# Constant columns written ahead of the loads, mask building reordered, and attention of batch 1 spread over ch1 and ch2 of batch 0

## The chip, the cores and the metric

The kernel runs on one core of a Trainium2 chip. The metric is the device time of one launch in microseconds (us). Each kernel was launched several times, and the median is quoted. A profile is one of those launches, recorded by the hardware profiler. The span in a profile is about 2 us shorter than the time of the same launch, so spans are compared with spans and times with times.

Engine names in profile lines: PE is TensorE (matmul), PEld its weight loads, DVE VectorE, ACT ScalarE, POOL GpSimd (here it issues the loads) and SP SyncE (it issues the stores).

## The reference

Eight batches, eight heads, 576 positions, head size 64: causal attention over a window of 128 positions with a distance bias, then an MLP mixer on the result. Inputs and outputs are float32.

```python
rel = pos[:, None] - pos[None, :]
mask = (rel >= 0) & (rel < 128)
attn = softmax(where(mask, scale * q @ k.T - slope * |rel|, -1e9))
x = (attn @ v)                                  # (batch, 576, 512)
h = np.maximum(xt @ w_tok1, 0.0) @ w_tok2       # xt: x transposed
u = x + h.transpose(0, 2, 1)
out = u + np.maximum(u @ w_ch1, 0.0) @ w_ch2    # d_ch = 1536
```

## The kernel before

Attention works on pairs of heads, four pairs to a batch, so batch 1 is pairs 4 to 7. A pair takes three steps. `att_T` transposes q and k on TensorE and copies both out of PSUM. `att_S(g, half)` makes scores, `exp` on ScalarE, and multiplies by a mask on VectorE (tile `pb`). `att_V` multiplies by v; v carries a column of ones, so the softmax sum comes with it, and VectorE divides (tile `xb`). All three take their PSUM tiles from one pool of two. `regroup(b, ...)` rearranges q and k of a batch on VectorE before its transposes.

The mixer of a batch is `tok1`, `tok2` (result `ub`), transposes (`ut`, copied to `UT`), `ch1` (24 groups of four matmuls, each followed by a Relu on ScalarE) and `ch2`. `mixer_items(b)` holds ch2 of batch b-1 and the rest of batch b. `spread(main, side)` interleaves two lists by cost.

```python
    with tc.manual_schedule():          # every engine keeps this order
        dma_qk(0, 0, 2)                 # GpSimd issues the loads: q, k, v of batch 0,
        ...                             # weights, q and k of batch 1, v of batch 1
        nc.vector.memset(patT[0 : P - TAIL, :], 0.0)
        nc.vector.memset(W1[0 : P - TAIL, NF, :], 0.0)
        nc.vector.memset(vp[0][0 : P - TAIL, NF, :, 0:D], 0.0)
        build_consts()
        regroup(0, 0, 2)
        build_bias()
        build_masks(0)
        att_T(0, True)
        regroup(0, 2, 4)
        att_S(0, 0)
        att_T(1, True)
        nc.vector.memset(vp[0][:, :, :, D : D + 1], 1.0)      # ones column, batch 0
        build_masks(1)
        ...                             # the other pairs of batch 0
        nc.vector.memset(vp[1][0 : P - TAIL, NF, :, 0:D], 0.0)
        nc.vector.memset(vp[1][:, :, :, D : D + 1], 1.0)      # ones column, batch 1

    with tc.manual_schedule(engines={ENG.PE}):   # only TensorE keeps this order
        its = mixer_items(0)
        n = len(its) - NHT
        run(its[:n])                    # mixer 0 up to the 12th ch1 group
        regroup(1, 0, H)
        ...
        side = []
        for g in range(NHP, 2 * NHP):   # batch 1: T and S, no V
            side.append((0.6, lambda g=g: att_T(g)))
            side.append((0.5, lambda g=g: att_S(g, 0)))
            side.append((0.5, lambda g=g: att_S(g, 1)))
        spread(its[n:], side)           # over the last 12 ch1 groups
        its = mixer_items(1, lead=3)
        run(its[:6])
        spread(its[6:9], [(0.6, lambda g=g: att_V(g)) for g in range(NHP, 2 * NHP)])
        its = its[9:]
        side = [(0.6, lambda: att_T(2 * NHP)), (0.6, lambda: att_T(2 * NHP + 1))]
        side += [(0.5, lambda: att_S(2 * NHP, 0)), (0.5, lambda: att_S(2 * NHP, 1))]
        for g in range(2 * NHP, 3 * NHP):
            side += att_step(g)         # T of pair g+2, S of g+1, V of g
        spread(its, side)
        ...                             # batches 2 to 8: spread(mixer_items(b), att_steps)
```

In the second block a scheduler puts the work of the other engines in order, so the place of an instruction on VectorE has to be looked up in the built program.

The softmax here doesn't subtract the row's maximum and nothing guards it: scores larger than these inputs give would overflow.

## Time and profile before

| kernel before | |
|---|---|
| median time | 357.11 us (356.5 to 357.9) |
| first tok1 matmul | 39.94 us |
| first ch1 matmul | 51.30 us |
| start of mixer 2 | 126.86 us |
| from there to the end | 229.6 us of a span of 356.5 |

The times within the span are starts of the named matmuls in the timeline. From mixer 2 on, TensorE has next to no waits (38.27 us busy of the 38.60 us from 127 to 165.6), so there was little to win there.

The table of busy time by stretches gives the middle of the kernel, from the first ch1 to mixer 2. After the stretch and its length come the busy time of each engine (with its instructions), the mean granted TensorE clock (the share of its full speed that the chip allowed), the DMA share and GB/s.

```profile
core 0: us, PE busy (x) PEld busy (x) DVE busy (x) ACT busy (x) POOL busy (x), PEclk, DMA share, GB/s
51.30:126.86 75.56, 63.72 (x637) 40.80 (x636) 37.43 (x61) 45.16 (x94) 8.13 (x10) 0.91 0.60 84
```

TensorE is busy 63.7 of 75.6 us, at a clock of 0.91.

The timeline of VectorE shows the start. Columns: start, duration, engine, line, operation, output<-input, and in brackets the idle time before it and what ended it.

```profile
16.65 0.43 DVE L169 COPY masks<-patB 128x512 bf16<-128x512 bf16 x1 [6.76 <-DMA vp_91<-in_v_dram]
16.78 0.09 DVE L505 MEMSET vp_91<- 128x40 bf16 x1
33.53 0.96 DVE L145 COPY qg<-qn_86 96x3072 bf16<-96x3072 bf16 x1 [6.65 <-DMA qn_86<-in_q_dram]
36.20 0.95 DVE L145 COPY kg<-kn_88 96x3072 bf16<-96x3072 bf16 x1 [0.39 <-DMA kn_88<-in_k_dram]
39.06 0.82 DVE L295 TENSOR_TENSOR xb<-ot,rt 128x640 bf16<-128x640 f32 x1
48.59 0.73 DVE L347 TENSOR_TENSOR ub<-ht,xb 128x512 bf16<-128x512 f32 x1 [1.33 <-DMA vp_92<-in_v_dram]
48.72 0.09 DVE L529 MEMSET vp_92<- 128x40 bf16 x1
```

The masks at 16.65 us need no load. They stand behind the ones column of `vp_91`, which had to wait for the loads into the same tile. (The profile starts the ones column 0.13 us after the masks; in the order of this block, which every engine keeps, it comes first.) In the same way the fourth `ub` addition, at 48.59 us, stands behind the ones column of `vp_92` (0.09 us of work), which waited for v of batch 1. Between them lies the regroup of batch 1, which waits for q and k. The chain of waits puts the two large DMA waits on the critical path:

```profile
17.65 13.00 DMA WC_105<-in_moe_w_ch_dram
31.58 16.84 DMA vp_92<-in_v_dram
```

The timeline of TensorE shows the waits of the middle stretch:

```profile
51.30 8.00 PE L371 MATMUL ct<-UT,WC_105 128*128 128x288 bf16 x52
61.34 0.39 PE L244 MATMUL sp<-qTz_93,kT_97 64*128 64x256 bf16 x4 [1.03 <-DVE kT_97 L222]
66.17 0.39 PE L244 MATMUL sp<-qTz_94,kT_98 64*128 64x256 bf16 x4 [1.92 <-DVE kT_98 L222]
71.01 0.39 PE L244 MATMUL sp<-qTz_95,kT_99 64*128 64x256 bf16 x4 [1.92 <-DVE kT_99 L222]
77.76 0.39 PE L244 MATMUL sp<-qTz_96,kT_100 64*128 64x256 bf16 x4 [2.29 <-DVE kT_100 L222]
92.51 1.24 PE L330 MATMUL t_971<-xb,W_103 128*128 128x512 bf16 x5 [1.78 <-DVE xb L295]
105.55 0.29 PE L356 MATMUL ut<-swap,ub 128*128 128x128 bf16 x1 [2.67 <-DVE ub L347]
126.86 0.39 PE L393 MATMUL o_1494<-ident,UT 128*128 128x128 bf16 x4
```

The first and the last line are the first ch1 and the start of mixer 2. The scores of each pair wait for the copy of its k, because T and S of one pair follow each other with only one ch1 group between.

### The profile page before, as it was taken

To read this page: it belongs to the slowest core of one execution; us is meant where nothing else is said; L and a number is where in the kernel's file an instruction comes from. 1 tells how busy PE (TensorE), PEld (TensorE's weight loads), DVE (VectorE), ACT (ScalarE), POOL (GpSimd) and SP (SyncE) were. 2 spreads that over 40 slices of the span, in tenths; PEclk is the share of its full clock that TensorE was granted. 3 is DMA by queue.
4 is the path that set the end of the run, shared out by engine and by line. 5 is a ranking of instruction groups with operands and counts; after the bars stand their busy time and mean duration, and the time that the engine had idled before them with its cause. 6 is when DMAs were issued, how large, how long until landed. Compare 5 with 4: busy or idle time off the path is not lost.

```text
span 356.5 us, 6716 instructions
## 1 busy us (share of the span) xinstructions
PE 310.6 (87%) x2816; PEld 190.8 (54%) x2816; DVE 180.1 (51%) x342; ACT 178.8 (50%) x373; POOL 59.5 (17%) x79
## 2 busy tenths in 40 slices
PE   2271768579779999999999999999999999999995
PEld 1051336345437754676457645674577457745842
DVE  5292450453587548733694368534953275326012
ACT  3462007760356963286439642784378425711810
POOL 8961250020401041004000400013000000000000
PEclk9999989969998999999999999999999999999999
DMA  7999999128903692905790391009110111002022
GB/s 95 129 179 205 190 139 201 16 31 162 98 32 41 94 82 59 180 31 36 92 158 35 25 104 59 31 2 97 41 52 0 31 59 61 2 31 73 16 61 89
DMA packets 59502, 27.76 MB, mean 78 GB/s; under 512 B 38672, under 2 KB 54864, under 8 KB 59472
## 3 DMA queue, kind: packets, MB, share of 16 engines
q0 software_dynamic: 54224, 17.90, 50.7%
q1 hardware_dynamic: 5248, 9.44, 7.8%
q8 instruction: 22, 0.36, 0.5%
q14 instruction: 8, 0.07, 0.1%
HBM read 35.78 MB, written 9.44 MB: 127 GB/s over the span
## 4 chain that ended last, share of the span: by engine, by line
PE 73%; DMA 8%; DVE 8%; POOL 5%; issue 3%; ACT 2%; POOLq 0%; DVEq 0%
PE ct L371 27%; DMA vp_92<-in_v_dram 5%; PE sp L244 5%; PE ot L287 4%; DMA WC_105<-in_moe_w_ch_dram 4%; PE tT L204 3%; PE ut L360 2%; DVE ub L347 2%; PE ht L343 2%; POOL vp_91 L137 2%; DVE kg L145 1%; PE o_829 L399 1%; DVE kT_100 L222 1%; ACT pe L258 1%; POOL kn_87 L119 1%
## 5 line engine op out<-in xcount | busy, mean ns | idle before, releaser
L371 PE MATMUL ct<-UT,WC_105 128*128 128x288 bf16 x768 | 107.8, 291 | 0.2
L258 ACT ACTIVATE pe<-sp,biascol 128x512 bf16<-128x512 f32 x128 | 81.3, 692 | 28.1 <-PE sp L244 28.0
L376 ACT ACTIVATE R_102<-ct 128x288 bf16<-128x288 f32 x192 | 73.8, 423 | 40.0 <-PE ct L371 34.1
L371 PEld LDWEIGHTS <-WC_105 128*128 128x128 bf16 x768 | 72.1, 99 | 23.4 <-issue 3.9
L265 DVE TENSOR_TENSOR pb<-pe,masks 128x1024 bf16<-128x1024 bf16 x64 | 44.0, 689 | 60.9 <-ACT pe L258 60.7
L399 PEld LDWEIGHTS <-R_102 128*128 128x128 bf16 x432 | 39.6, 98 | 42.9 <-issue 2.6
L287 PEld LDWEIGHTS <-pb 128*128 128x128 bf16 x576 | 23.5, 103 | 12.1 <-issue 7.2
L347 DVE TENSOR_TENSOR ub<-ht,xb 128x512 bf16<-128x512 f32 x40 | 25.9, 682 | 7.0 <-PE ht L343 5.7
L131 POOL DMA_DIRECT2D vp_92<-in_v_dram x16 | 14.2, 899 | 77.1 <-PE ot L287 70.1
L295 DVE TENSOR_TENSOR xb<-ot,rt 128x640 bf16<-128x640 f32 x32 | 26.4, 824 | 1.0
L343 PE MATMUL ht<-r1t,W_104 128*128 128x512 bf16 x80 | 21.7, 379 | 1.6 <-DVE ub L347 1.1
L204 PEld LDWEIGHTS <-qg 96*128 96x128 bf16 x192 | 12.2, 103 | 19.2 <-DVE qg L145 14.3
L287 PE MATMUL ot<-vp_91,pb 128*128 128x65 bf16 x288 | 13.7, 209 | 7.8 <-DVE xb L295 6.6
L131 POOL DMA_DIRECT2D vp_91<-in_v_dram x12 | 10.5, 889 | 44.4 <-PE ot L287 40.3
L330 PEld LDWEIGHTS <-W_103 128*128 128x128 bf16 x80 | 7.9, 103 | 13.1 <-issue 6.2
L365 DVE COPY UT<-ut 128x576 bf16<-128x576 bf16 x32 | 13.2, 452 | 2.4 <-PE ut L360 2.3
L215 ACT COPY qTz_96<-tT 128x576 bf16<-128x576 bf16 x7 | 4.5, 639 | 18.2 <-PE tT L204 18.1
L343 PEld LDWEIGHTS <-W_104 128*128 128x128 bf16 x80 | 7.3, 98 | 11.0 <-issue 3.9
L215 ACT COPY qTz_93<-tT 128x576 bf16<-128x576 bf16 x7 | 4.5, 639 | 15.5 <-PE tT L204 15.3
L204 PE MATMUL tT<-ident,qg 96*128 96x96 bf16 x168 | 12.0, 208 | 0.0
L204 PE MATMUL tT<-ident,kg 96*128 96x96 bf16 x168 | 11.9, 208 | 0.0
L222 DVE COPY kT_97<-tT 128x576 bf16<-128x576 bf16 x7 | 5.3, 758 | 13.0 <-ACT qTz_93 L215 13.0
(186 smaller groups left out, 367.6 us busy)
## 6 DMA issues: line engine op xcount, KB each, us to landing
out_dram<-obt SPq DMA_DIRECT2D x32, 256.0 KB, 2.0
qn_86<-in_q_dram POOLq DMA_DIRECT2D x4, 576.0 KB, 9.7
kn_88<-in_k_dram POOLq DMA_DIRECT2D x4, 576.0 KB, 11.6
vp_92<-in_v_dram POOLq DMA_DIRECT2D x16, 128.0 KB, 5.2
qn_85<-in_q_dram POOLq DMA_DIRECT2D x3, 576.0 KB, 6.8
kn_87<-in_k_dram POOLq DMA_DIRECT2D x3, 576.0 KB, 9.9
WC_105<-in_moe_w_ch_dram POOLq DMA_DIRECT2D x3, 512.0 KB, 10.1
WC_106<-in_moe_w_ch_dram POOLq DMA_DIRECT2D x1, 1536.0 KB, 23.7
```

The lines of the kernel that those rows point to most:

```text
L131: nc.gpsimd.dma_start(out=vp[b % 2][:, c, :, 0:D], in_=v[b, :, c * P : (c + 1) * P, :].rearrange("h s d -> s h d"),)
L204: nc.tensor.transpose(tt[n][:, j * RP : (j + 1) * RP], t_raw[:RP, j, 2 * hp : 2 * hp + 2, :].rearrange("p h d -> p (h d)"), ident[:RP, :RP],)
L244: nc.tensor.matmul(sp[:, hh, i * 256 + x0 : i * 256 + x1], lhsT=kt[r, k0 : k0 + P], rhs=qz[r, 0, q0 : q0 + x1 - x0], start=True, stop=True,)
L258: nc.scalar.activation(out=pe[:, i, :].rearrange("p (k x) -> p k x", k=2), in_=sp[:, i, :].rearrange("p (k x) -> p k x", k=2) if ROW_TILED ...
L265: nc.vector.tensor_tensor(out=pb[:, :, :], in0=pe[:, :, :], in1=masks[:, half, 2 * hp : 2 * hp + 2, :], op=ALU.mult,)
L287: nc.tensor.matmul(ot[:, i, qb * (D + 1) : (qb + 1) * (D + 1)], lhsT=pb[:, i, col : col + P], rhs=vb[:, kc, h, :], start=(n == 0), stop=(n ...
L295: nc.vector.tensor_tensor(out=xb[b][:, :, 2 * hp * D : (2 * hp + 2) * D].rearrange("p c (i d) -> p i c d", i=2), in0=o4[:, :, :, 0:D], in1 ...
L343: nc.tensor.matmul(ht[:, :], lhsT=W2[:, j, c0(c) : c0(c) + P], rhs=r1s[b, j][:, :], start=(j == 0), stop=(j == NDH - 1),)
L347: nc.vector.tensor_tensor(out=ubs[b][:, c, :], in0=ht[:, :], in1=xb[b][:, c, :], op=ALU.add)
L371: nc.tensor.matmul(ct[:, :], lhsT=WC1[:, cb, ht_i * P : (ht_i + 1) * P], rhs=UT[:, cb, o : o + SH], start=(cb == 0), stop=(cb == NCB - 1),)
L376: nc.scalar.activation(out=R2[:, ht_i, o : o + SH], in_=ct[:, :], func=ACT.Relu)
L399: nc.tensor.matmul(o2[0][:, :], lhsT=R2[:, ht_i, col : col + P], rhs=WC2[:, ht_i, :], start=(ht_i == 0 and c != NF), stop=(ht_i == NHT - 1),)
```

## The change

Its intent: no VectorE instruction that needs no data should stand behind one that does, and batch 1's attention should run as the same pipeline as later batches' (T two pairs ahead, S one ahead, then V). Cut to its core; a branch of the kernel that was never taken was also removed, and the loads of q and k are given out one batch earlier, which leaves GpSimd's order unchanged except that q and k of batch 2 come before v of batch 2.

```diff
     with tc.manual_schedule():
+        for i in range(2):
+            nc.vector.memset(vp[i][:, :, :, D : D + 1], 1.0)
+            nc.vector.memset(vp[i][0 : P - TAIL, NF, :, 0:D], 0.0)
+        nc.vector.memset(W1[0 : P - TAIL, NF, :], 0.0)
+        nc.vector.memset(patT[0 : P - TAIL, :], 0.0)
         dma_qk(0, 0, 2)
 ...
-        (the same memsets, one by one, among the pairs of batch 0 and after them)
         build_consts()
         regroup(0, 0, 2)
         build_bias()
+        att_T(0, True)
         build_masks(0)
-        att_T(0, True)
         regroup(0, 2, 4)
         att_S(0, 0)
         att_T(1, True)
         build_masks(1)
-        regroup(0, 4, 6)
         att_S(0, 1)
+        regroup(0, 4, 6)
         att_S(1, 0)
         att_T(2, True)
         build_masks(2)
-        regroup(0, 6, 8)
         att_S(1, 1)
-        att_V(0)
+        regroup(0, 6, 8)
 ...     (V of pairs 0 and 1 one step later each)
     with tc.manual_schedule(engines={ENG.PE}):
-        (run mixer 0; T and S of batch 1; run ch2; V of batch 1)
+        its0, its1 = mixer_items(0), mixer_items(1, lead=3)
+        n0, n1 = len(its0) - NHT, 9
+        run(its0[:n0])
+        side = [(0.0, lambda: regroup(1, 0, H))]
+        if B > 3:
+            side.append((0.0, lambda: dma_qk(3, 0, H)))
+        for g in range(NHP - 2, 2 * NHP):
+            side += att_step(g, NHP)
+        spread(its0[n0:] + its1[:n1], side)
         side = []
         for g in range(2 * NHP, 3 * NHP):
             side += att_step(g)
+        spread(its1[n1:], side)
```

More of the change, by code (lines that the diff above doesn't have):

```diff
@@ L14 @@
 TPP = 6
-ROW_TILED = True
 def spread(main, side):
@@ L95 @@
     NR = 4
-    qTz = [
-        const.tile([P, 1 if ROW_TILED else 2, S], bf16, name=f"qTz{i}") for i in range(NR)
-    ]
+    qT = [const.tile([P, S], bf16, name=f"qT{i}") for i in range(NR)]
     kT = [const.tile([P, S], bf16, name=f"kT{i}") for i in range(NR)]
@@ L208, in att_T, with nat @@
                 )
-        def nat(rows, n):
-            return tt[n][rows, 0:S].rearrange("c (j p) -> c p j", j=TPP)
+        def nat(n):
+            return tt[n][:, 0:S].rearrange("c (j p) -> c p j", j=TPP)
         def dst(a):
-            return a.rearrange("c (p j) -> c p j", j=TPP)
-        qz, kt = qTz[g % NR], kT[g % NR]
-        if ROW_TILED:
-            nc.scalar.copy(out=dst(qz[:, 0, :]), in_=nat(slice(0, P), 0))
-        else:
-            nc.scalar.copy(out=dst(qz[0:D, 0, :]), in_=nat(slice(0, D), 0))
-            nc.scalar.copy(out=dst(qz[D:P, 1, :]), in_=nat(slice(D, P), 0))
-        if early:
-            nc.scalar.copy(out=dst(kt[:, :]), in_=nat(slice(0, P), 1))
-        else:
-            nc.vector.tensor_copy(out=dst(kt[:, :]), in_=nat(slice(0, P), 1))
+            return a[:, :].rearrange("c (p j) -> c p j", j=TPP)
+        nc.scalar.copy(out=dst(qT[g % NR]), in_=nat(0))
+        (nc.scalar.copy if early else nc.vector.tensor_copy)(out=dst(kT[g % NR]), in_=nat(1))
         if hp == NHP - 1 and 0 < b < B - 1:
             regroup(b + 1, 0, H)
-            if b + 2 < B:
-                dma_qk(b + 2, 0, H)
+            if b + 3 < B:
+                dma_qk(b + 3, 0, H)
     def att_S(g, half):
         b, hp = divmod(g, NHP)
-        qz, kt = qTz[g % NR], kT[g % NR]
+        qt, kt = qT[g % NR], kT[g % NR]
         sp = ps_at.tile([P, 2, 512], f32, name="sp", tag="at")
@@ L240, in att_S @@
             for x0, x1, k0, q0 in mms:
-                if ROW_TILED:
-                    for hh in range(2):
-                        r = slice(hh * D, (hh + 1) * D)
-                        nc.tensor.matmul(
-                            sp[:, hh, i * 256 + x0 : i * 256 + x1],
-                            lhsT=kt[r, k0 : k0 + P], rhs=qz[r, 0, q0 : q0 + x1 - x0],
-                            start=True, stop=True,
-                        )
-                else:
+                for hh in range(2):
+                    r = slice(hh * D, (hh + 1) * D)
                     nc.tensor.matmul(
-                        sp[:, i, :].rearrange("p (h x) -> p h x", h=2)[:, :, x0:x1],
-                        lhsT=kt[:, k0 : k0 + P], rhs=qz[:, :, q0 : q0 + x1 - x0],
+                        sp[:, hh, i * 256 + x0 : i * 256 + x1],
+                        lhsT=kt[r, k0 : k0 + P], rhs=qt[r, q0 : q0 + x1 - x0],
                         start=True, stop=True,
@@ L258, in att_S @@
             nc.scalar.activation(
-                out=pe[:, i, :].rearrange("p (k x) -> p k x", k=2),
-                in_=sp[:, i, :].rearrange("p (k x) -> p k x", k=2) if ROW_TILED
-                else sp[:, :, 256 * i : 256 * (i + 1)],
-                func=ACT.Exp, bias=biascol[:, h : h + 1], scale=scale,
+                out=pe[:, i, :], in_=sp[:, i, :], func=ACT.Exp, bias=biascol[:, h : h + 1], scale=scale,
             )
@@ L308, with att_step @@
     NG = B * NHP
-    def att_step(g):
+    def att_step(g, g0=0):
         its = []
-        if g + 2 < NG:
+        if g0 <= g + 2 < NG:
             its.append((0.6, lambda: att_T(g + 2)))
-        if 0 <= g + 1 < NG:
+        if g0 <= g + 1 < NG:
             its.append((0.5, lambda: att_S(g + 1, 0)))
             its.append((0.5, lambda: att_S(g + 1, 1)))
-        if 0 <= g < NG:
+        if g0 <= g < NG:
             its.append((0.6, lambda: att_V(g)))
@@ L485 @@
             dma_v(1, c)
-        def zero_q(i):
-            if not ROW_TILED:
-                nc.vector.memset(qTz[i][D:P, 0, :], 0.0)
-                nc.vector.memset(qTz[i][0:D, 1, :], 0.0)
-        zero_q(0)
-        nc.vector.memset(patT[0 : P - TAIL, :], 0.0)
-        nc.vector.memset(W1[0 : P - TAIL, NF, :], 0.0)
-        zero_q(1)
-        nc.vector.memset(vp[0][0 : P - TAIL, NF, :, 0:D], 0.0)
         build_consts()
@@ L504 @@
         att_T(1, True)
-        nc.vector.memset(vp[0][:, :, :, D : D + 1], 1.0)
         build_masks(1)
-        zero_q(2)
+        att_S(0, 1)
         regroup(0, 4, 6)
-        att_S(0, 1)
         att_S(1, 0)
-        zero_q(3)
         att_T(2, True)
         build_masks(2)
+        att_S(1, 1)
         regroup(0, 6, 8)
-        att_S(1, 1)
-        att_V(0)
+        if B > 2:
+            dma_qk(2, 0, H)
         att_S(2, 0)
@@ L520 @@
         att_S(2, 1)
+        att_V(0)
+        att_S(3, 0)
         att_V(1)
-        att_S(3, 0)
         att_S(3, 1)
@@ L527 @@
         nc.vector.tensor_copy(out=swap[:, TAIL:P], in_=ident[:, 0:TAIL])
-        nc.vector.memset(vp[1][0 : P - TAIL, NF, :, 0:D], 0.0)
-        nc.vector.memset(vp[1][:, :, :, D : D + 1], 1.0)
     def run(its):
@@ L535 @@
     with tc.manual_schedule(engines={ENG.PE}):
-        its = mixer_items(0)
-        n = len(its) - NHT
-        run(its[:n])
-        regroup(1, 0, H)
-        if B > 2:
-            dma_qk(2, 0, H)
-        side = []
-        for g in range(NHP, 2 * NHP):
-            side.append((0.6, lambda g=g: att_T(g)))
-            side.append((0.5, lambda g=g: att_S(g, 0)))
-            side.append((0.5, lambda g=g: att_S(g, 1)))
-        spread(its[n:], side)
-        its = mixer_items(1, lead=3)
-        run(its[:6])
-        spread(its[6:9], [(0.6, lambda g=g: att_V(g)) for g in range(NHP, 2 * NHP)])
-        its = its[9:]
-        side = [(0.6, lambda: att_T(2 * NHP)), (0.6, lambda: att_T(2 * NHP + 1))]
-        side += [(0.5, lambda: att_S(2 * NHP, 0)), (0.5, lambda: att_S(2 * NHP, 1))]
+        its0, its1 = mixer_items(0), mixer_items(1, lead=3)
[7 more added lines that the diff above has]
+        spread(its0[n0:] + its1[:n1], side)
+        side = []
         for g in range(2 * NHP, 3 * NHP):
             side += att_step(g)
-        spread(its, side)
+        spread(its1[n1:], side)
         for b in range(2, B + 1):
```

## The prediction

> **What bounds the kernel now** (timeline, chain of waits, busy table by stretches).
>
> 1. 0 to 51.2 us, until the first ch1 matmul: TensorE is busy 22 us of it. The chain of waits is DMA: weights land at 30.7 us, q and k of batch 1 at 33.5 and 36.2, v of batch 1 at 48.4. The ones column of v (batch 0) makes VectorE idle 6.8 us until 16.65 us; that of batch 1 waits until 48.4, and the fourth ub addition starts only then. VectorE also idles from 26.9 to 33.5 us behind the regroup of batch 1.
> 2. 51.2 to 127 us: ch1 and ch2 of batch 0, all of mixer 1. TensorE is busy 64 of 75.8 us. From 59 to 79.6 us a head pair's T and S take about 4.8 us for 12 ch1 matmuls (1.5 us warm): copy of q (0.64), of k (0.76), S, exp twice (1.27), on two PSUM buffers. V of batch 1 comes in a lump (86 to 92 us), then tok2 stalls (100 to 109 us).
> 3. 127 to 340 us: 36 to 38 us per batch, TensorE over 99% busy. The change leaves it alone.
>
> **What the change does.**
> - Ones and zero columns go first (about 1.2 us of VectorE, where it is idle). Both waits on v vanish.
> - VectorE works through 9.9 to 16.7 us. By the instruction order, though, the regroup of batch 1 still stands ahead of the last pb and xb of batch 0, and its data land at 33.5 and 36.2 us, by an unchanged DMA order. So most of the 6.8 us is given back: after k lands, regroup 0.95 + xb 0.82, so tok1 starts near 38.1 us instead of 39.9. tok2 without the v wait saves 1.4 us more: the first ch1 starts near 48 us, 3.2 us gained.
> - Batch 1 attention becomes a pipeline (T two pairs ahead, S one, V) over the last 12 ch1 and first 9 ch2 items. Twelve leading ch1 groups still run alone, the first 4 cold: four matmuls take 0.96 us there against 0.49 later. The Trainium skill ("TensorE: Matmul & The Clock Gate", Part 1) says that a TensorE that idled restarts at half rate; this trace agrees.
>
> Estimate of phase 2: leading ch1 8 us. Then 12 x 0.49 + 9 x 0.86 = 13.6 us main and about 10 us attention, 24 us if TensorE were full; ScalarE needs about 12 x 0.43 + 5.5 x 3.2 = 23 us, and each pair claims a PSUM buffer four times for some 2 us, with two buffers: over 4 us a pair. So it is bound by latency, 27 us (near 5 us a pair). Rest of mixer 1 with attention of batch 2: about 31 us (now 35.3, with two T and one S more). 66 us instead of 75.8: mixer 2 starts near 114 us, not 127.
>
> **On the critical path:** 3 us from the start, 10 from phase 2. 357.1 - 13 = 344 us. Range 338 to 350. Chances: faster 0.91, same 0.08, slower 0.01.
>
> **What would show it.** VectorE never waits for v; tok1 at 37.5 to 38.5 us, first ch1 near 48; VectorE still idle before 33.5 us on q of batch 1; V interleaved with ch2; TensorE fuller between 48 and 114 us; later batches still 36 to 38 us.
>
> **What would make it wrong.** PSUM buffers or ScalarE turn round slower in the dense stretch (6 us a pair: 5 us less gain). VectorE copies during 10 to 17 us slow GpSimd's issuing of v and shift all loads. The regroup of batch 2 waits for its DMA. Or stalls vanish fully (near 337).

## The result, and the profile after

The changed kernel takes 346.43 us (345.94 to 346.77), the kernel before 357.11 us: a ratio of 0.9699 (95% interval 0.9676 to 0.9721). A ratio here is the mean time of one kernel's fast runs over that of the other's fast runs of the same rounds, so it is not quite the ratio of the medians. The prediction was 344, range 338 to 350.

| | before | after | predicted |
|---|---|---|---|
| first tok1 matmul | 39.94 | 38.62 | 38.1 |
| first ch1 matmul | 51.30 | 48.53 | 48 |
| start of mixer 2 | 126.86 | 114.82 | 114 |
| first ch1 to mixer 2 | 75.56 | 66.29 | 66 |
| span | 356.5 | 344.5 | |

Of the 12.0 us between the two spans, 2.8 come from the start and 9.3 from the middle; from mixer 2 on they take 229.6 and 229.7 us. The launch profiled before was a slower one (358.36 us), which is why the medians lie only 10.7 us apart.

The middle in the table by stretches, after:

```profile
48.53:114.82 66.29, 58.75 (x638) 39.32 (x635) 37.73 (x62) 45.47 (x95) 10.41 (x14) 0.97 0.90 104
```

The same work takes 5 us less of TensorE's busy time, because the clock is 0.97 instead of 0.91: one stretch at half clock is left, from 95.2 us, where there were four. VectorE and ScalarE do what they did; GpSimd issues 14 loads there instead of 10.

VectorE's timeline at the start, after:

```profile
34.20 0.96 DVE L142 COPY qg<-qn_86 96x3072 bf16<-96x3072 bf16 x1 [10.59 <-DMA qn_86<-in_q_dram]
36.94 0.89 DVE L142 COPY kg<-kn_88 96x3072 bf16<-96x3072 bf16 x1
37.76 0.81 DVE L275 TENSOR_TENSOR xb<-ot,rt 128x640 bf16<-128x640 f32 x1
44.26 3.08 DVE L327 TENSOR_TENSOR ub<-ht,xb 128x512 bf16<-128x512 f32 x5 [5.52 <-PE ht L323]
```

No line waits for v any more, and the five `ub` run in one piece. But the idle time before the regroup grew from 6.65 to 10.59 us: VectorE did its masks early and then waited for q of batch 1, with the last `xb` of batch 0 in line behind. tok1 needs that `xb`.

TensorE's timeline of the middle, after:

```profile
48.53 7.13 PE L351 MATMUL ct<-UT,WC_105 128*128 128x288 bf16 x52
64.07 0.72 PE L267 MATMUL ot<-vp_92,pb 128*128 128x65 bf16 x18
69.75 0.71 PE L267 MATMUL ot<-vp_92,pb 128*128 128x65 bf16 x18
82.33 1.24 PE L310 MATMUL t_1025<-xb,W_103 128*128 128x512 bf16 x5 [2.03 <-DVE xb L275]
83.92 1.24 PE L310 MATMUL t_1048<-xb,W_103 128*128 128x512 bf16 x5
95.86 0.29 PE L336 MATMUL ut<-swap,ub 128*128 128x128 bf16 x1 [3.70 <-DVE ub L327]
114.82 0.39 PE L373 MATMUL o_1496<-ident,UT 128*128 128x128 bf16 x4
```

V of batch 1 comes one pair at a time. The four waits for a copy of k, of up to 2.3 us each, are gone (0.3 us is the longest left). The two waits of mixer 1, for `xb` and for `ub`, are still there and have grown, from 1.78 to 2.03 us and from 2.67 to 3.70 us.

### The profile page after: what moved, and what is told of

Its sections match the earlier page's. It is cut to its first block, busy times and chain, and to the rows that moved or that the text cites. A ratio compares the mean times of both kernels' runs of the same rounds, so it can differ in the third digit from the quotient of the medians.

```text
span 344.5 us, 6712 instructions
## 1 busy us (share of the span) xinstructions
PE 305.8 (89%) x2816; PEld 188.8 (55%) x2816; DVE 179.2 (52%) x342; ACT 178.7 (52%) x373; POOL 59.9 (17%) x79
## 4 chain that ended last, share of the span: by engine, by line
PE 74%; DVE 11%; POOL 5%; DMA 4%; ACT 3%; issue 2%; POOLq 0%; ACTq 0%
PE ct L351 27%; PE sp L233 4%; DMA qn_86<-in_q_dram 4%; PE ot L267 4%; PE tT L201 3%; DVE ub L327 3%; PE ht L323 2%; PE ut L340 2%; POOL vp_91 L134 2%; ACT pe L241 2%; DVE kg L142 2%; DVE qg L142 1%; DVE kT_100 L211 1%; DVE xb L275 1%; DVE obt L391 1%
## 5 line engine op out<-in xcount | busy, mean ns | idle before, releaser
L351 PE MATMUL ct<-UT,WC_105 128*128 128x288 bf16 x768 | 104.0, 286 | 0.2
L351 PEld LDWEIGHTS <-WC_105 128*128 128x128 bf16 x768 | 71.3, 98 | 22.1 <-issue 3.5
L379 PEld LDWEIGHTS <-R_102 128*128 128x128 bf16 x432 | 39.0, 98 | 41.6 <-issue 1.5
L310 PEld LDWEIGHTS <-W_103 128*128 128x128 bf16 x80 | 7.9, 103 | 14.0 <-issue 7.2
L323 PEld LDWEIGHTS <-W_104 128*128 128x128 bf16 x80 | 7.4, 99 | 11.1 <-issue 4.2
## 6 DMA issues: line engine op xcount, KB each, us to landing
kn_88<-in_k_dram POOLq DMA_DIRECT2D x4, 576.0 KB, 10.7
```

The lines of the kernel that those rows point to most:

```text
L323: nc.tensor.matmul(ht[:, :], lhsT=W2[:, j, c0(c) : c0(c) + P], rhs=r1s[b, j][:, :], start=(j == 0), stop=(j == NDH - 1),)
L351: nc.tensor.matmul(ct[:, :], lhsT=WC1[:, cb, ht_i * P : (ht_i + 1) * P], rhs=UT[:, cb, o : o + SH], start=(cb == 0), stop=(cb == NCB - 1),)
L379: nc.tensor.matmul(o2[0][:, :], lhsT=R2[:, ht_i, col : col + P], rhs=WC2[:, ht_i, :], start=(ht_i == 0 and c != NF), stop=(ht_i == NHT - 1),)
```

## The experiments

Eleven kernels were run, each with a profile and three timed rounds; all gave the right output. Runs were made in three groups, each beside its own runs of the kernel before (medians 357.79, 357.46 and 357.08 us). "Middle" is first ch1 to mixer 2; "clock" is its mean granted TensorE clock. The columns "first ch1", "middle" and "clock" come from one profiled launch each. e4_pipe, e7_pipe_fill and e11_before_fill have the start of the kernel before, and their first ch1 falls anywhere from 50.97 to 51.71 us, so differences of under 0.8 us at the start say nothing.

| run | median us | ratio to before | first ch1 | middle | clock |
|---|---|---|---|---|---|
| before | 357.11 | 1 | 51.30 | 75.56 | 0.91 |
| changed | 346.43 | 0.9699 | 48.53 | 66.29 | 0.97 |
| e1_memset | 352.54 | 0.9857 | 47.16 | 73.17 | 0.93 |
| e2_reorder | 358.57 | 1.0036 | 53.08 | 73.64 | 0.93 |
| e3_start | 353.80 | 0.9899 | 47.81 | 73.77 | 0.93 |
| e4_pipe | 352.65 | 0.9857 | 51.71 | 69.50 | 0.93 |
| e5_late | 336.42 | 0.9408 | 37.93 | 66.46 | 0.97 |
| e6_fill | 344.39 | 0.9629 | 48.22 | 65.22 | 1.00 |
| e7_pipe_fill | 349.19 | 0.9780 | 51.58 | 65.18 | 0.99 |
| e8_delay | 348.04 | 0.9736 | 49.62 | 66.38 | 0.97 |
| e11_before_fill | 353.82 | 0.9917 | 50.97 | 71.69 | 0.98 |
| e9_late_fill | 333.68 | 0.9349 | 37.28 | 65.19 | 1.00 |
| e10_regroup | 330.69 | 0.9267 | 37.09 | 63.47 | 1.00 |

### Which part carries the gain: e1 to e4

My theory gave about 3 us to the constant columns, nothing to the mask reordering, and the rest to the new placing of batch 1. The rivals: the reordering carries the start, or the placing needs the early start.

e1_memset, constant columns alone, on the kernel before:

```diff
     with tc.manual_schedule():
+        for i in range(2):
+            nc.vector.memset(vp[i][:, :, :, D : D + 1], 1.0)
+            nc.vector.memset(vp[i][0 : P - TAIL, NF, :, 0:D], 0.0)
+        (W1 and patT likewise; the later memsets removed)
```

> The kernel before with only the constant columns of v (and the two small clears) moved ahead of the loads. My theory: the start alone is worth 2.7 us. Without the waits for v the scheduler also puts the regroup of batch 1 later in VectorE's order, so tok1 starts near 38.5 us instead of 39.9, no ub addition waits for v, and the first ch1 starts near 48.5 us instead of 51.3: time 354.3 us (353.5 to 355). Rival, that the mask reordering is needed for the gain at the start: under 1 us gained, 356.5. GpSimd's eight issues of v of batch 0 should take 6.8 us as in the changed kernel if VectorE's work in that time is what slows them, 6.0 as before if not.

Measured: 352.54 us, 5.3 us faster than the kernel before of the same rounds, more than expected. tok1 starts at 37.37 us and the first ch1 4.1 us earlier than before. The scheduler moved the regroup of batch 1 later by itself, as foreseen, and q of batch 1 landed 0.8 us earlier than before instead of later. A further 2.4 us come from the middle, whose order did not change; its clock went from 0.91 to 0.93, because the half-clock stretch from 50.9 us, behind the wait for `ub`, is gone. (Together that is 6.5 us between the profiles and 5.3 between the medians, since the profiled launch of the kernel before was a slower one.) GpSimd's eight issues took 6.09 us, not 6.8, though VectorE was busy 6.3 of the 7 us from 8.2 to 15.2. So a busy VectorE is not enough to slow them. In the changed kernel, where they took 6.84 us, one issue of the eight took 1.60 us and the others 0.75 to 0.83 us, while the first mask copy beside it took 0.28 us; in e1_memset no issue took over 0.87 us, and the mask copies beside the last two took 0.60 and 0.56 us. It looks as if now the one engine and now the other were held up; why it falls out one way or the other stays open. The price is at most 0.8 us.

e2_reorder, order of the first block alone:

```diff
-        build_masks(0)
         att_T(0, True)
+        build_masks(0)
 ...     (the block as in the change, with the memsets left where they were)
```

> The kernel before with only the order of the first block changed (masks before regroup, V of batch 0 later), the constant columns where they were. My theory: no gain, since the ones column of batch 0 still holds VectorE until 16.7 us and that of batch 1 still holds the ub additions until 48.4 us; the second to fifth ub now come after it, so the first ch1 starts near 52 us: 357 to 358.5 us. Rival, that the reordering carries the gain at the start: 354.5. The eight issues of v take 6.0 us, because VectorE idles then.

Measured: 358.57 us, ratio 1.0036 (1.0007 to 1.0064). No gain, a slight loss: the second `ub` now waits for v until 48.4 us and the other three follow it. (Its middle is shorter because the first half-clock stretch now falls mostly ahead of the first ch1; mixer 2 starts at 126.72 us, as before.) The eight issues took 5.97 us, as expected.

e3_start, both together:

```diff
+        (memsets first, as in e1_memset)
+        (order of the block as in e2_reorder)
```

> Both changes of the start, without the new placing of batch 1 attention. My theory: same as the constant columns alone, 354.3 us within 0.5; first ch1 near 48.5 us. Rival, that reordering and constant columns add up: 352 or less.

Measured: 353.80 us, ratio 0.9899 (0.9874 to 0.9923), against 0.9857 (0.9836 to 0.9879) for e1_memset. Adding the reordering to the constant columns gains nothing and seems to cost about 1 us; the intervals overlap a little.

e4_pipe, the new placing alone (the changed kernel with the first block of the kernel before):

```diff
-        (memsets first; new order of the first block)
+        (first block of the kernel before)
```

> The changed kernel with the start of the kernel before: only the placing of batch 1 attention is new. My theory: first ch1 near 51.3 us, from there to the start of mixer 2 66.3 us as in the changed kernel instead of 75.5: 348 us (347 to 349.5), so that the two parts add up to the whole. Rival, that the placing needs the early start: over 350.

Measured: 352.65 us, ratio 0.9857 (0.9837 to 0.9876). That is over 350, so by the mark that I had set, the rival has it: the placing gains more with the early start than without. The whole start (e3_start) and the placing multiply to 0.9899 x 0.9857 = 0.976 against 0.970 for the whole change, which gains 2 us more than its parts. The placing alone gains 5.1 us in time where I expected about 9. Its middle is the changed kernel's, instruction for instruction on TensorE, and takes 69.50 us instead of 66.29. TensorE's timeline shows where:

```profile
85.52 1.62 PE L310 MATMUL t<-xb,W 128*128 128x512 bf16 x5 [2.03 <-DVE xb L275]
87.90 2.11 PE L310 MATMUL t<-xb,W 128*128 128x512 bf16 x5
103.50 3.06 PE L351 MATMUL ct<-UT,WC 128*128 128x288 bf16 x12
107.08 1.63 PE L351 MATMUL ct<-UT,WC 128*128 128x288 bf16 x12
```

The five tok1 matmuls after the wait of 2.03 us take 1.62 and 2.11 us, where the changed kernel's take 1.24 after the same wait; twelve ch1 matmuls after the second wait take 3.06 us, the next twelve 1.63 (the changed kernel's first twelve 1.64, after the same wait of 3.70 us). The granted clock fell after these waits. The Trainium skill ("TensorE: Matmul & The Clock Gate", Part 1) describes this gate: half rate after an idle window of about 3.4 us, full rate after a busy one, and a window that runs freely. The clock records of my traces agree: in all 13 profiles the clock changes only at steps of 3.41 us, and these steps do not keep their place to the start of the kernel from one profile to another. The table by stretches, cut at the steps, shows what they do to the wait of 2.03 us, first in e4_pipe (wait from 83.5 to 85.5 us), then in the changed kernel (from 80.3 to 82.3 us):

```profile
82.82:86.23 3.41, 1.38 (x23) 0.92 (x22) 2.61 (x5) 0.89 (x2) 2.66 (x4) 1.00 0.35 84
86.23:89.65 3.42, 3.42 (x20) 1.73 (x18) 0.76 (x1) 1.24 (x2) 1.54 (x2) 0.50 2.25 143
78.14:81.55 3.41, 1.91 (x28) 1.24 (x28) 2.31 (x6) 2.38 (x4) 1.17 (x2) 1.00 0.04 11
81.55:84.97 3.42, 2.64 (x22) 1.38 (x21) 0.91 (x2) 1.15 (x2) 3.03 (x4) 1.00 1.62 162
```

In e4_pipe the whole wait lies in one window; TensorE is busy 1.38 of 3.41 us, and the next window runs at half clock. In the changed kernel a step divides the wait, the two windows are busy 1.91 and 2.64 us, and the clock stays up. Counted over all 13 profiles, from the first clock record of each (at 31.5 to 45.4 us) and with the busy time that the profiles show, the busy share of a window decides without exception: the 21 full-clock windows with a half-clock window after them were busy at most 43.9%, the 1106 others at least 44.3%. The second wait, of 3.70 us, costs the clock in both kernels, but in e4_pipe for two windows: the first slow one was busy only 2.59 of 3.41 us (76%), and in the 21 slow windows after which the clock came back it was at least 81%.

### The clock: e6, e7, e8, e11

Dummy matmuls, whose results nobody reads, fill TensorE's waits. If a wait only costs its own length, they change nothing.

e6_fill, on the changed kernel:

```diff
+    def warm(n):
+        wt = ps_ma.tile([P, DM], f32, name="warm", tag="ma")
+        for i in range(n):
+            nc.tensor.matmul(wt[:, :], lhsT=ident[:, :], rhs=WC2[:, 0, :], start=True, stop=True)
 ...
+            if b == 1:
+                its.append((0.0, lambda: warm(7)))      # ahead of tok1
 ...
+            if b == 1:
+                its.append((0.0, lambda: warm(14)))     # ahead of the transposes
```

> The changed kernel with dummy matmuls (results unused) put where TensorE waits in mixer 1: 7 ahead of tok1 (wait of 2.0 us) and 14 ahead of the transposes (wait of 3.7 us). They cost nothing if they end before the wait does. Theory that the clock lost in these waits is real time: cycles lost from first ch1 to mixer 2 fall from 2.0 us to under 0.7, time 345 us (344.3 to 346). Rival, that the clock record is not tied to time here: 346.4 or more.

Measured: 344.39 us, about 2 us faster than the changed kernel, the clock of all its runs 1.0. The waits are still there, filled:

```profile
79.83 1.67 PE L400 MATMUL warm<-WC,ident 128*128 128x512 bf16 x7
82.02 1.24 PE L310 MATMUL t<-xb,W 128*128 128x512 bf16 x5 [0.52 <-DVE xb L275]
91.79 3.19 PE L400 MATMUL warm<-WC,ident 128*128 128x512 bf16 x14
95.56 0.23 PE L336 MATMUL ut<-swap,ub 128*128 128x128 bf16 x1 [0.58 <-DVE ub L327]
```

The first transpose takes 0.23 us instead of 0.29. More work made the kernel faster, so the slow clock after a wait costs real time: here 1.1 us of the middle (66.29 to 65.22).

e7_pipe_fill, the same on e4_pipe:

```diff
+        (warm(7) ahead of tok1 and warm(14) ahead of the transposes of batch 1, on e4_pipe)
```

> New placing alone with the start of before, as in e4_pipe (352.65 us, granted clock 0.93 from first ch1 to mixer 2), plus the same dummy matmuls. Theory that e4_pipe fell 3.2 us short of its part only by the clock after these two waits: clock over 0.98 there, the stretch 65 to 66 us instead of 69.5, time 348.5 to 349.5 us. Rival, that something else in the late start costs it: 352 to 353.

Measured: the middle takes 65.18 us, 4.3 less, at a clock of 0.99. So the shortfall of e4_pipe was the clock. The time is 349.19 us, but its four runs spread from 347.5 to 351.4, the slower ones at a mean clock of 0.99 over the whole run, the others at 0.995 and 1.0.

e8_delay, the changed kernel with a later start:

```diff
         att_V(2)
+        nc.vector.memset(scratch[:, :], 0.0)     # 128 x 2048 float32
         att_V(3)
```

> The changed kernel with one VectorE memset of about 2.1 us ahead of the last xb of batch 0, so tok1 starts 2.1 us later and all that follows is the same. If time follows the start alone: 348.5 us. Theory that the clock after a wait also depends on when the wait falls: the stretch from first ch1 to mixer 2 changes from 66.3 us by up to 3 us either way at the same full-clock length of 64.3 us, so the time may be anywhere from 347 to 352.

Measured: 348.04 us. Half of the memset hid behind the wait for k: tok1 and ch1 start 1.0 and 1.1 us later than in the changed kernel. The middle is 66.38 us at 0.97, the same. This shift did not move the clock, and e4_pipe's shift of 3.2 us goes with 0.93. The windows tell why: in e8_delay a step divides the wait of 2.03 us again (the two windows are busy 55% and 85%), in e4_pipe the wait lies in one. A shift of under 1 us can decide, and launches of the same kernel differ too: the four launches of the changed kernel have a mean clock of 0.995 twice and 0.99 twice. How many windows are lost is in part chance.

e11_before_fill, dummies in the kernel before:

```diff
             side.append((0.6, lambda g=g: att_T(g)))
+            side.append((0.0, lambda: warm(6)))
             side.append((0.5, lambda g=g: att_S(g, 0)))
+        (also warm(6) ahead of tok1 and warm(11) ahead of the transposes of batch 1)
```

> The kernel before with dummy matmuls (results unused) in the waits of its second phase: 6 ahead of each pair's first S of batch 1, 6 ahead of tok1 of batch 1, 11 ahead of its transposes. In the kernel before that phase takes 75.6 us at a granted clock of 0.91, 68.8 us at full clock (time times clock). Theory that about half of what the new placing gains is clock: the phase shrinks to 69 to 71 us with no change of its order, time 351 to 352.5 us. Rival, that the clock loss falls only into waits and the placing is worth it all: 356.5 or more.

Measured: 353.82 us, ratio 0.9917 (0.9885 to 0.9949). The middle:

```profile
50.97:122.66 71.69, 67.05 (x671) 41.97 (x676) 37.14 (x61) 44.79 (x94) 8.12 (x10) 0.98 0.64 89
```

Without any change of order, warmth alone takes 3.9 us off the middle. My estimate of 69 to 71 us was too low: it came from multiplying time by clock (75.56 x 0.91 = 68.8), which counts slow cycles inside waits as lost although they cost nothing; and one half-clock stretch is left, from 50.0 to 53.5 us, behind the wait ahead of the first transposes, where I had put no dummies. Filled, the old placing takes 71.7 us (e11_before_fill) and the new one 65.2 (e6_fill). Of these 6.5 us, 0.6 are the stretch that is left: the twelve leading ch1 groups take 7.6 us in e11_before_fill and 7.0 in e6_fill. So of the 9.3 us of the middle about 5.9 are the order itself and about 3.4 the clock. The dummies can lengthen a wait a little (the first scores of batch 1 come 0.2 us later after the transposes than before), so the split holds to some tenths of a us.

### What the start still waits for: e5, e9, e10

The prediction said that most of what VectorE gains early is given back behind the regroup of batch 1. e5_late takes that regroup out of the way, on the changed kernel:

```diff
+    with tc.manual_schedule():          # all engines keep this order
+        run(its0[:n00])                 # tok1, tok2, transposes of batch 0
+        regroup(1, 0, H)
     with tc.manual_schedule(engines={ENG.PE}):
-        run(its0[:n0])
-        side = [(0.0, lambda: regroup(1, 0, H))]
+        run(its0[n00:n0])               # the first 12 ch1 groups
+        side = []
```

> The changed kernel with one move: token mixing and transposes of batch 0 are kept in strict order, and the regroup of batch 1, which waits for q and k until 34.2 and 37 us, comes after them on VectorE. My theory (the early V of batch 0 is given back behind that regroup): tok1 starts near 25 us instead of 38.6, first ch1 near 34 to 36 us instead of 48.5, then the loads of batch 1 (v near 49 us) hold a little: 332 us (330 to 337). Rival, that tok1 is held by its weights or by v, not by the order: within 2 us of the changed kernel's 346.4.

Measured: 336.42 us, ratio 0.9408 (0.937 to 0.9445). VectorE's timeline:

```profile
27.04 0.82 DVE L275 TENSOR_TENSOR xb<-ot,rt 128x640 bf16<-128x640 f32 x1
33.65 3.09 DVE L327 TENSOR_TENSOR ub<-ht,xb 128x512 bf16<-128x512 f32 x5 [5.61 <-PE ht L323]
38.76 0.95 DVE L142 COPY qg<-qn 96x3072 bf16<-96x3072 bf16 x1
39.63 0.95 DVE L142 COPY kg<-kn 96x3072 bf16<-96x3072 bf16 x1
```

tok1 starts at 27.92 us instead of 38.62, first ch1 at 37.93 instead of 48.53; the middle is unchanged (66.46). So the place of the regroup on VectorE held the whole start for 10.6 us: all that tok1 needed could be there by 27.9 us. (The edit keeps a strict order on all engines; that the gain is the regroup's is read from the idle time of 10.59 us ahead of it in the changed kernel, which is gone here.) I had expected tok1 near 25 us: the attention of batch 0 is itself done only at 27.9 us.

e9_late_fill adds the dummies of e6_fill to e5_late:

```diff
+        (e5_late with warm(7) and warm(14) as in e6_fill)
```

> e5_late plus the dummy matmuls of e6_fill. If the two gains add up (10.0 and 2.0 us off the changed kernel): 334.4 us, clock over 0.99 from first ch1 to mixer 2, that stretch 65.2 us instead of 66.5. If the earlier start takes away the waits that were filled: 336.4.

Measured: 333.68 us, ratio 0.9349 (0.9321 to 0.9377); the gains add up.

e10_regroup, built on e9_late_fill, also gives out the regroup of each later batch elsewhere, and has 5 dummies instead of 14 ahead of the transposes, since the wait should be shorter:

```diff
-        if hp == NHP - 1 and 0 < b < B - 1:      # in att_T
+        if hp == 1 and 0 < b < B - 1:            # in att_V
             regroup(b + 1, 0, H)
```

> e9_late_fill with the regroup of the next batch given out at V of pair 1 instead of T of pair 3, so that in mixer 1 the two regroup copies (1.7 us on the chain) come after the ub additions and the copies of the transposes; only 5 dummies ahead of the transposes, since the wait should fall from 3.7 us to about 2. Theory that the wait for ub in mixer 1 is VectorE's order: stretch from first ch1 to mixer 2 63.5 to 64 us, time 332.5 to 333.5. Rival, that the wait is the ub additions' own length: 334.4.

Measured: 330.69 us, ratio 0.9267 (0.9235 to 0.93). VectorE's timeline in mixer 1, first of the changed kernel, then of e10_regroup:

```profile
91.53 0.75 DVE L211 COPY kT_100<-tT 128x576 bf16<-128x576 bf16 x1
92.20 0.94 DVE L142 COPY qg<-qn_86 96x3072 bf16<-96x3072 bf16 x1
93.06 0.95 DVE L142 COPY kg<-kn_88 96x3072 bf16<-96x3072 bf16 x1
93.93 1.88 DVE L327 TENSOR_TENSOR ub<-ht,xb 128x512 bf16<-128x512 f32 x3
```

```profile
80.10 0.74 DVE L211 COPY kT<-tT 128x576 bf16<-128x576 bf16 x1
80.76 1.87 DVE L327 TENSOR_TENSOR ub<-ht,xb 128x512 bf16<-128x512 f32 x3
83.18 1.55 DVE L345 COPY UT<-ut 128x576 bf16<-128x576 bf16 x4
84.65 0.95 DVE L142 COPY qg<-qn 96x3072 bf16<-96x3072 bf16 x1
```

The last three `ub` no longer stand behind 1.7 us of copies that nobody needs yet, and the middle takes 63.47 us. The fewer dummies are no rival for this gain: both sets end before the wait does (0.57 us before the first transpose in e9_late_fill, 0.78 in e10_regroup). It is the fastest kernel here, 4.5% faster than the changed one (0.9267 / 0.9699 = 0.955). It still carries twelve dummy matmuls; real work in those places would be the better filling, which was not tried.

## Why the prediction was right

The time was 346.43 us, inside the range and 2.4 us above the 344 predicted.

- **Waits on v vanish: right.** No wait of VectorE for v is left. Alone this is worth more than the 3 us I put down: e1_memset gains 5.3 us in time; its profile has 4.1 us at the start and 2.4 in the middle, where a half-clock stretch went with the wait.
- **What VectorE gains early is given back: right.** Idle time before q of batch 1 rose to 10.59 us, the reordering alone gained nothing (1.0036), and taking the regroup out of the way started tok1 10.7 us earlier.
- **tok1 at 38.1, ch1 at 48, mixer 2 at 114 us: right** within 0.9 us (38.62, 48.53, 114.82).
- **Twelve leading ch1 groups in 8 us, the first cold: off.** They took 7.0 us (48.53 to 55.50), since the wait ahead of their transposes was 1.45 us instead of 2.92 and left the clock up.
- **The stretch "bound by latency, 27 us": right size, wrong reason.** From 55.50 to 82.33 us it took 26.8 us, but TensorE was busy 23.2 of them. The longest wait, 2.03 us, was the one for the last `xb` ahead of tok1. The 23.2 us are close to the 24 us that the prediction gave for a full TensorE. Latency of the PSUM buffers showed only in waits of at most 0.6 us. That the size came out is luck.
- **"Rest of mixer 1 ... about 31 us": short by 1.5.** It took 32.5 us. The prediction took 4.3 us off the 35.3 us of before and gave no term to the wait for `ub`, 2.67 us there. That term failed: the wait did not shrink but grew to 3.70 us, because the regroup of batch 3 stands ahead of the last three `ub` additions (e10_regroup moved it and gained), and slow matmuls followed it.
- **The clock as a term of its own: missing.** Apart from the first ch1 groups I counted waits and added them. The filled pair shows that about 3.4 of the 9.3 us are clock, and e4_pipe that the same placing gains only 6.1 us of the middle (75.56 to 69.50) when more windows are lost. That the middle came out at 66.3 us, with 66 predicted, is in part luck.
- **13 us in all:** the two profiles differ by 12.0 us, as added up; the medians by 10.7, because the profiled launch of the kernel before was one of its slower ones.
- **Later batches unchanged: right.** 38.6 and 36.1 us for the first two, as before.

## What to carry to other kernels

On an in-order engine, look at what stands behind each instruction that waits for a load. A memset of 0.09 us and a regroup of 1.9 us held work that was ready, and moving the second one was worth almost as much as the whole change (10.0 us against 10.7). Before you judge how much a reordering can gain, follow what it frees up to the next wait on the same engine: the constant columns of batch 0 freed 6.8 us of VectorE, and tok1 started only 2.6 us earlier (e1_memset). Waits of 2 us on TensorE can cost more than their length, since the matmuls after them can run slow; here that took a window of 3.41 us with TensorE busy under 44%. Dummy matmuls in the waits are a cheap way to measure how much.

## What the Trainium skill lacked or had wrong

- "TensorE: Matmul & The Clock Gate", Part 1, gives an idle window of about 3.4 us for the drop to half rate, and no busy share at which a window counts as idle. In the 13 profiles here every full-clock window with TensorE busy 43.9% or less was followed by half clock, and none with 44.3% or more. So the wait of 2.03 us in e4_pipe, amid matmuls of attention, cost the clock (the five matmuls after it took 1.62 us, the next five 2.11, instead of 1.24), and the same wait in the changed kernel, divided by a window's end, did not. Nor does the page say how busy a slow window must be for the clock to come back: 76% was not enough, 81% was.
- The same page puts the ramp at under 1% of a typical span and says nothing of filling waits with unread matmuls. Here they gained 0.8% on the kernel before (ratio 0.9917), about 1% on e4_pipe (352.65 to 349.19 us) and about 0.6% on the changed kernel (346.43 to 344.39 us), the last two between medians of different rounds.
